# One fused attention and MLP kernel, five engines in a written-out order: the order of all operations and the identity products replaced

## The chip, the cores and the metric

The kernel runs on one core of a Trainium2 chip. The metric is the device time of one execution in microseconds (us); the kernel before was run three times and its median is 237.82 us. Engines are named as in the profile: PE (TensorE, matrix products), DVE (VectorE), ACT (ScalarE), POOL (GpSimd) and SP (SyncE, which only issues DMAs here).

## The reference, cut to what matters

Each of 4 x 8 heads has a sequence of 768 positions of 64 numbers, cut into 8 blocks of 96. An 8 x 8 matrix P per head is normalised five times by rows and columns. Blocks of k and v are mixed with P, and each block of q attends to the mixed block of its own index alone. The result, 3072 tokens of 512 numbers, goes through an MLP with a leaky slope per hidden unit.

```python
for _ in range(5):
    P = np.exp(P - np.max(P, axis=-1, keepdims=True))
    P = P / (np.sum(P, axis=-1, keepdims=True) + 1e-09)
    P = P / (np.sum(P, axis=-2, keepdims=True) + 1e-09)
k_sorted = np.einsum('bhij,bhjcd->bhicd', P, k_b)
v_sorted = np.einsum('bhij,bhjcd->bhicd', P, v_b)
attn = softmax(scale * q_b @ k_sorted_b.T)          # inside one block of 96
x = (attn @ v_sorted_b) -> [3072, 512]
h = x @ w_in                                        # [3072, 2048]
g = np.maximum(h, 0.0) + alpha * np.minimum(h, 0.0)
out = g @ w_out                                     # [3072, 512]
```

## The kernel before

The kernel has two layers. The function `bass_sinkhorn_attn__then__act_prelu_kernel` adds some 1230 operations to a graph (`G.add`), each with the buffers that it reads and writes; an operation is one instruction, or a few that belong together. The table `SEQ` then gives the order: it lists the number of every operation once, and `arrange` puts each at the end of its engine's list as it comes. A letter behind a number (p, a, d) chooses POOL, ACT or DVE for an operation that may run on several. `emit` writes each engine's list with the semaphore waits that the buffers ask for. Every engine works its list strictly in order. The durations and priorities that `G.add` also takes are read by neither `arrange`, `warm` nor `emit`: with the table given, no instruction depends on them.

The table `WARM` puts identity products into PE's list: `89:14:y` means 14 products of the identity with itself, 512 columns each, ahead of operation 89, into the PSUM bank `psY`. Their results are never read (line 808 is their product; four more of them are an operation of the graph).

The work, by the lines that the profile shows:

- q, k and v of batch 0 and both weight matrices are loaded by DMAs that POOL issues (L397, L419, L908 for w_in in four pieces, L913 for w_out in two). They follow each other in one queue.
- P is normalised on DVE and ACT in a chain of small operations (L518 to L532). The product L539 spreads the result over partitions, and DVE makes from it the block matrix BDK (L543).
- For batch 0, the products L600 transpose q and mix k, in six groups of 16 each; L653 copies v into an order that the products L674 can read, in eight copies that POOL or DVE may do; ACT and DVE bring results out of PSUM into QTz, KT and VS (L372).
- Attention of block g: scores (L715 in the first eight blocks, L712 later), the row maximum on DVE (L721), in the first eight blocks a second round of products with the maximum subtracted (L736, L727) and the exponential ET (L759); later the exponential per head (L748) and a DMA transpose of its result, issued by SP. Then the output product (L768), its division by the sum (L776, L779) and a transpose to xT, by PE (L794) or by a DMA from SP.
- The later batches' k and v are mixed through KSz and VDz (copies L616 and L658, products L629 and L669), their q comes through QN (L401) and DMA transposes.
- MLP: L823 computes a group of 128 hidden units for 192 tokens (the first two chunks, two blocks each) or 384 tokens (later), four products to a group, into one of three PSUM banks at first and one of two later. ACT takes the negative part (L833), DVE puts both parts together into hT (L836), which frees the bank. L863 computes 128 tokens of the output in four groups of four products; the first two of these need the first half of w_out. ACT or DVE copies the result out (L372), and SP stores it.

Of the kernel before, what the change touches and what calls it, by code (L numbers as in the profile page):

```python
# [7 lines left out]
AP = bass.AP  # L8
# [17 lines left out]
VSL = 4  # L26
# [6 lines left out]
89:14:y 79:8:y 93:2:y 104:2:y 158:6:y 118:1:y 128:4:y 162:1:y 153:3:h 205:1:y 207:1:y  # L33
# [3 lines left out]
0 7 11 2 3 1 4 8 9 22 42 28 14 43 44 45 46 19 47 18 5 48 49 50 15 51 39 52 53 6 54 55 25 56 138 57 58 23 29 59 12p  # L37
60 61 130 62 63 64 31 65 32 66 37 13 67 68 89 69 83 81 70 84 71 87 131 10 91 88 85 132 72 40 73 90 74 133 75 86 76
41 77 82 134 78 79 92 26 80 147 93 148 102 94d 103a 104 95 105a 100 98 96a 99a 97d 109d 106p 35 111d 112d 108p 34
16 101a 36 38 33 107p 158 149 114 115d 146 110p 118 250p 159 116 248p 119a 120 113p 121d 124 30 117d 160 135 125a  # L40
249p 254p 24 136 161 122 137 144 150 126 127a 143 123d 145 128 151 129d 253p 247d 20 17 152 162 21 163 164 141 153
177 154 140 155 165 156 142 166d 184 157a 167 185 196 193 168 186 169 194 197 195 199 198 187 202 170 27 203 205
200 204 188 201 214 206 220 215 217 189 218 207 221 219 222 226 216 229 190 227 223 230 273 228 224 171 208 231 225
235 191 236 238 192a 237 232 239 261 251 262 209 313p 233 252a 240 210 263 347p 211 139 255 241 270 234 212 403 264
256a 213d 291 404 301d 271 242 175 259 292 258p 274 260a 257p 272 265 352p 267 243 266 279 244 311p 293 280 268
300p 281 282 269 312p 294 245 174 304d 285 310p 246d 275 286 351p 283 287 284 338 348p 302 339 295 305p 303a 314
288 296 315 306 289 316 340 307a 290 176 297 320 341 317 276 318 178 321 319 298 322 379 299a 308 380 323 179 309a
342 326 324 343 349 344 327 381 350a 325 328 345 353 382 346d 329 354d 332 330 383 333 331 357 277a 334 180 335
572p 384 361 385 336 402 373 362 337 360p 358a 183 363 419 359d 574p 386 364 420 391p 367 365 374 355p 368 366 421
356d 573p 182 388 387d 370 389d 395p 375 577p 369 371 392 390p 435 372 393a 429 394p 436 396 430 376 397d 437 422  # L50
445p 431 432 578p 377d 398 446p 181 453 399d 447p 405 454 449p 433 438 455 465 448p 400 434 459 401a 466 456 460
451 461 457 406 467 452d 483 458 415 423 450d 477 462 475p 478a 172 468 424 413 495 476d 463 407 425 484 418 378
496 408 411 464 481 409d 412 482a 486 485 426 479p 549 487 427d 497 480p 488 439 506p 507 440 492 508d 509p 489 414
441 493 498 511 494 505p 490 442 525 443a 491 516 510p 512a 417 526 513 517 278 535p 537 518 514 469 550 571p 527
515 416 470 519 471 536p 522 538d 520 528 472 561 523 521 539 473a 562 543 540a 499 524 428 544 541 551 563 500 501
546 534 542d 502 545 575 503a 597 576d 474 547 555 548 529 556 606 530 558 564 607a 612p 557 552 609p 531 559 608p
560 610 553a 579 444 638p 613d 611a 582 598 580 532 635 583 591 637d 599 581 570 636d 585 584 592 586 600 533a 639
587 588 640a 626 589 614 646 627 644 641 615 565 590 593 643 628 566 645 616 617 642d 620 567 618 629 594 621 619
622 677 595a 504 568 623 678 569a 659 624 601 410 660 662 602 679 554 603 663 625 661 604 668 605a 680 718p 704 669
671 713p 705 714p 664 672 706 673 665 670 630 719 631 674 666a 632 752p 707 648 686 675 649 633 676 692 687 667  # L60
748p 634a 716d 596 720a 739 688 681 650 689 749d 715p 717d 698 690 647 750 691 658 699 693 751a 700 652 701 173 740
721 778p 702 682 753p 694 703 722 741 723 695 754 724 755d 696a 742 727 683 725 779 726 728 733 729 768 848d 730
854p 769 777p 756 731 812p 780a 708 732 654 734 757 709 782d 770 655 783 758 735 784d 657 762 710 813p 771 759 763
651 743 764 760 814 736 849p 711 815a 761 656 781d 803 744 847p 785 737d 684 850p 804 765 786 853p 653 788 766 805
767 789 787 794 745 797 806 838 798 816 839 772 697 817a 790 795 738 799 818 840 746 791 773 796 774 820 819d 775
800 792a 807 801 851 793 826 821 802 852a 841 822 873 823 874 832 824 747 881 833 827 888p 882a 834 846 875 828 825
808 855 884d 685 809 885 835 856 883d 911p 886a 857 842 887p 836 829 912p 837 712 909 843 830a 861 858 831 862 910a
901 863 876 867 859 860 889 811 902 913 890 864 891 868 865 844 903 869 914d 866 895 915 904 896 892 897 870 893
810 916a 894 877 871a 917 935 776 918 898 936 920 899 919 937 921 900 878 879 929 926 880 961 927 905 962 930 922
938 928 981 963 931 923 906 907 845 932 943 933 964 987 934 944 982 924d 908 988 939 946 945 983 989 940 941 949  # L70
# [960 lines left out]
```

## Time and profile before

| what | value |
|---|---|
| three runs | 237.7, 237.82, 238.86 us |
| span of the profiled execution (first to last instruction) | 236.6 us |
| PE busy, granted clock | 229.2 us, 1.000 |
| DVE busy | 169.8 us |
| ACT busy | 151.6 us |
| POOL busy | 73.0 us |
| moved by DMA | 31.36 MB in 71453 packets |

The profiled execution gives its span; what lies around the span is not in it, and the median of the runs is 1.2 us above it. In the profile a matrix product's time includes its latency, so neighbours overlap: the distance of two starts is what a product costs PE. A row of the timeline gives the start, the time, engine, line, what is written and read, and in brackets the idle time before it with what ended it.

### The profile page before, as it was taken

What the parts mean: (1) busy time and instruction counts of PE and PEld (TensorE: products, weight loads), DVE (VectorE), ACT (ScalarE), POOL (GpSimd) and SP (SyncE); (2) the same over time, 40 slices, a digit from 0 to 9 for tenths busy, and PEclk for the clock granted to TensorE, in tenths of its full rate; (3) what the DMA queues carried; (4) which work ended last, traced back from release to release, by engine and by line L of the source; (5) the groups of instructions that cost most, each with busy time, mean ns of one, the idle gap of its engine ahead of it and who ended that gap; (6) DMA issues with size and microseconds to landing.
All of it is one profiled execution on the core that took longest, in us unless ns stands there. A gap on an engine that the chain in (4) does not pass through costs nothing.

```text
span 236.6 us, 6266 instructions
## 1 busy us (share of the span) xinstructions
PE 229.2 (97%) x2532; PEld 142.2 (60%) x2532; DVE 169.8 (72%) x354; ACT 151.6 (64%) x423; POOL 73.0 (31%) x139
## 2 busy tenths in 40 slices
PE   7998998999999999999999999999999999999995
PEld 3446676687666666556566665655555555555543
DVE  4748796989899997868887667676766587744350
ACT  4475265587887988886678786756864646453332
POOL 7958812915659620338590020000000000000000
PEclk9999999999999999999999999999999999999999
DMA  5999999999989999899998796542642323400033
GB/s 96 212 213 168 211 217 202 179 209 158 191 88 167 152 120 173 119 210 166 165 111 114 188 164 135 98 90 52 125 92 82 97 50 79 140 0 1 0 133 135
DMA packets 71453, 31.36 MB, mean 133 GB/s; under 512 B 64504, under 2 KB 65280, under 8 KB 71424
## 3 DMA queue, kind: packets, MB, share of 16 engines
q0 software_dynamic: 22896, 13.63, 42.0%
q1 hardware_dynamic: 48528, 17.33, 37.8%
q8 instruction: 20, 0.33, 0.5%
q14 instruction: 9, 0.07, 0.1%
HBM read 27.28 MB, written 6.29 MB: 142 GB/s over the span
## 4 chain that ended last, share of the span: by engine, by line
PE 76%; DMA 17%; POOL 6%; issue 1%; ACT 0%; POOLq 0%
PE psH L823 31%; PE psYP L863 28%; DMA w_out_bf<-in_moe_w_out_dram 10%; PE psS L863 3%; PE psS L712 3%; DMA VST<-in_v_dram 3%; PE psO L768 3%; PE psYP L669 2%; DMA ET<-Esb 2%; PE psYP L629 1%; DMA QTz<-QN 1%; POOL w_in_bf L908 1%; PE psO L863 1%; PE psS L727 1%; POOL VDz L456 1%; PE psO L794 1%
## 5 line engine op out<-in xcount | busy, mean ns | idle before, releaser
L836 DVE SCALAR_TENSOR_TENSOR hT<-t,omaT,psH 128x384 bf16<-128x384 f32 (+1 forms) x139 | 77.4, 571 | 36.6 <-ACT t L833 35.1
L823 PE MATMUL psH<-xT,w_in_bf 128*128 128x384 bf16 (+1 forms) x556 | 96.9, 311 | 0.0
L833 ACT ACTIVATE t<-psH 128x384 f32<-128x384 f32 (+1 forms) x139 | 63.1, 461 | 50.3 <-PE psH L823 49.2
L863 PE MATMUL psYP<-w_out_bf,hT 128*128 128x512 bf16 x336 | 83.2, 379 | 1.3 <-DMA w_out_bf<-in_moe_w_out_dram 1.3
L823 PEld LDWEIGHTS psH<-xT,w_in_bf 128*128 128x128 bf16 x556 | 49.5, 98 | 28.9 <-DVE hT L836 1.6
L863 PEld LDWEIGHTS psYP<-w_out_bf,hT 128*128 128x128 bf16 x336 | 30.8, 98 | 30.1 <-DMA w_out_bf<-in_moe_w_out_dram 1.8
L748 ACT ACTIVATE Esb<-psS,nf 96x96 bf16<-96x96 f32 x192 | 46.1, 345 | 2.0 <-DVE nf L721 2.0
L721 DVE TENSOR_REDUCE nf<-psS 96x8 f32<-96x768 f32 x24 | 22.8, 951 | 6.4 <-PE psS L712 6.0
L658 POOL COPY VDz<-VST 64x192 f32<-64x192 f32 x39 | 20.4, 524 | 20.3 <-DMA VST<-in_v_dram 16.6
L779 DVE TENSOR_TENSOR xq<-psO,rec 96x512 bf16<-96x512 f32 x31 | 21.2, 683 | 0.5
L401 POOL DMA_DIRECT2D QN<-in_q_dram x24 | 19.8, 833 | 3.3 <-DMA QTz<-QN 2.7
L616 POOL COPY KSz<-KS 64x256 f32<-64x256 f32 x28 | 11.1, 397 | 31.6 <-PE psYP L629 19.8
L712 PEld LDWEIGHTS psS<-KT,QTz 128*96 128x96 bf16 x192 | 12.1, 124 | 3.3 <-DMA QTz<-QN 0.2
L768 PEld LDWEIGHTS psO<-VS,ET 112*128 112x128 bf16 x248 | 11.1, 98 | 3.6 <-ACT ET L759 0.2
L808 PE MATMUL psYP<-identb 128*128 128x512 bf16 x40 | 12.8, 453 | 0.4 <-ACT identb L372 0.4
L372 ACT ACTIVATE VS<-psYP 112x512 bf16<-112x512 f32 x15 | 10.3, 687 | 4.2 <-PE psYP L669 2.2
L768 PE MATMUL psO<-VS,ET 112*128 112x65 bf16 x248 | 12.7, 194 | 0.0
L712 PE MATMUL psS<-KT,QTz 128*96 128x96 bf16 x192 | 12.6, 208 | 0.0
L372 ACT ACTIVATE KT<-psYP 128x512 bf16<-128x512 f32 x15 | 9.0, 599 | 2.8 <-PE psYP L629 1.8
L669 PEld LDWEIGHTS psYP<-BDV,VDz 128*128 128x128 bf16 x192 | 8.2, 98 | 2.7 <-POOL VDz L658 0.4
L372 ACT ACTIVATE outstg<-psYP 128x512 f32<-128x512 f32 x13 | 7.7, 604 | 3.2 <-PE psYP L863 3.2
L669 PE MATMUL psYP<-BDV,VDz 128*128 128x64 bf16 x192 | 9.5, 193 | 0.2 <-POOL VDz L658 0.2
(137 smaller groups left out, 198.8 us busy)
## 6 DMA issues: line engine op xcount, KB each, us to landing
out_dram<-outstg SPq DMA_DIRECT2D x23, 256.0 KB, 2.5
KS<-in_k_dram POOLq DMA_DIRECT2D x3, 768.0 KB, 13.3
QN<-in_q_dram POOLq DMA_DIRECT2D x24, 96.0 KB, 4.4
w_in_bf<-in_moe_w_in_dram POOLq DMA_DIRECT2D x4, 512.0 KB, 17.3
w_out_bf<-in_moe_w_out_dram POOLq DMA_DIRECT2D x2, 1024.0 KB, 23.9
VST<-in_v_dram POOLq DMA_DIRECT2D x4, 384.0 KB, 17.6
hT<-in_q_dram POOLq DMA_DIRECT2D x1, 768.0 KB, 7.6
VST<-in_v_dram POOLq DMA_DIRECT2D x1, 768.0 KB, 11.1
```

Source lines behind the costliest of these rows:

```text
L372: return e.activation(o, i, ACTF.Copy) if e is nc.scalar else e.tensor_copy(o, i)
L658: G.add(SHIFT, lambda e, o2=o2, i2=i2: e.tensor_copy(o2, i2), {"dve": 424, "pool": 525}, r=vst, w=[("VDz", u % VSL, th)], prio=prio)
L669: inst = e.matmul(AP(t, off + dd * 64, [[row, 128], [1, 64]]), AP(VDz, (u % VSL * 4 + dd // 2) * 256 + dd % 2, [[VSL * 1024, 128], [2, 128]]),
L712: inst = e.matmul(o, AP(QTz[n], hp * 3072 + h4 * 768 + i * 96, [[6144, 128], [1, 96]]), AP(KT[n], (h4 * 8 + i) * bk, [[ld, 128], [64, 2], ...
L721: G.add(DVE, lambda e: e.tensor_reduce(AP(nx, 0, [[8, 96], [4, 2], [1, 4]]), AP(psX, 0, [[1024, 96], [512, 2], [96, 4], [1, 96]]), AxisLis ...
L748: inst = e.activation(AP(Esb[me], p * 128, [[1024, 96], [64, 2], [1, 48]]), AP(psX, (p // 4) * 512 + (p % 4) * 96, [[1024, 96], [48, 2], [ ...
L768: inst = e.matmul(AP(psZ, hp * 512 + h4 * 68, [[1024, 128], [1, 65]]), AP(ET[me] if far else ET[m], pos(h4, hp) * 96, [[800, nk], [1, 128] ...
L779: G.add(DVE, lambda e: e.tensor_tensor(out=AP(xq[me], 0, [[512, 96], [256, 2], [64, 4], [1, 64]]), in0=AP(psZ, 0, [[1024, 96], [512, 2], [ ...
L823: inst = e.matmul(AP(pt, poff, [[1024, 128], [1, n]]), AP(w_in_bf, kt * DFF + ft // 2 * 256 + ft % 2, [[KT_TILES * DFF, 128], [2, 128]]), ...
L833: G.add(ACT, lambda e: e.activation(AP(t1[tb], 0, [[384, 128], [1, n]]), AP(pt, poff, [[1024, 128], [1, n]]), ACTF.Relu, scale=-1.0), t_ac ...
L836: G.add(DVE, lambda e: e.scalar_tensor_tensor(out=AP(hT, ft * RING + tok % RING, [[FT_TILES * RING, 128], [1, n]]), in0=AP(t1[tb], 0, [[38 ...
L863: inst = e.matmul(AP(bank[0], bank[1], [[1024, 128], [1, n]]), AP(hT, ft * RING + tok % RING, [[FT_TILES * RING, 128], [1, 128]]), AP(w_ou ...
```

## The change

The two tables SEQ and WARM are replaced by new ones, and many durations in `G.add` by others. All operations, loads and buffers stay. In the diff below, SEQ is cut to the first line of each; of the durations two are shown.

```diff
 WARM = """
-89:14:y 79:8:y 93:2:y 104:2:y 158:6:y 118:1:y 128:4:y 162:1:y 153:3:h 205:1:y 207:1:y
+79:7:y 118:8:y 156:1:i 202:1:q 291:1:y
 """

 SEQ = """
-0 7 11 2 3 1 4 8 9 22 42 28 14 43 44 45 46 19 47 18 5 48 49 50 15 51 39 52 53 6 54 55 25 56 138 57 58 23 29 59 12p
...
+0 7 2 10 3 1 4 11 12d 5 8 42 43 9 6 44 45 138 46 47 26 48 25 49 50 131 35 51 40 52 53 54 55 56 57 58 59 60 61 62
...
-        G.add(PE, s1, 395, r=kt_keys + qt_keys + [("xq", 1)] * (g == 2),
+        G.add(PE, s1, 357 if far else 215, r=kt_keys + qt_keys + [("xq", 1)] * (g == 2),
...
-                5000 if g < 18 else 3100, r=[("Esb", me)], w=[("ET", me), ("turned", g)], prio=prio, dma=(d_e[me], 0))
+                950, r=[("Esb", me)], w=[("ET", me), ("turned", g)], prio=prio, dma=(d_e[me], 0))
```

WARM holds 43 identity products before and 18 now (with the four of the graph, 47 and 22). The new file is one line longer ahead of all its functions, so that a line of it is one higher than the same line before: L824 now is L823 before.

At PE's start, before, the row of psS products that multiply bz is a burst of small products, and psS, psH and psO<-identb,hT transpose q:

```order
L889 MATMUL psS<-bz 32x32 x130
L808 MATMUL psYP<-identb 128x512 x14
L600 MATMUL psS<-identb,hT 64x64 x16
L600 MATMUL psH<-identb,hT 64x64 x32
L600 MATMUL psO<-identb,hT 64x64 x16
L600 MATMUL psS<-identb,hT 64x64 x16
L600 MATMUL psO<-identb,hT 64x64 x16
L808 MATMUL psYP<-identb 128x512 x8
L539 MATMUL psYP<-Pb,sel 128x8 x8
```

The same place of PE's list now:

```order
L890 MATMUL psS<-bz 32x32 x130
L601 MATMUL psH<-identb,hT 64x64 x16
L601 MATMUL psS<-identb,hT 64x64 x32
L601 MATMUL psO<-identb,hT 64x64 x32
L809 MATMUL psYP<-identb 128x512 x7
L540 MATMUL psYP<-Pb,sel 128x8 x8
```

The 14 identity products ahead of the q products are gone; between these and the spreading of P stand seven instead of eight, and one of the six q groups has gone behind the spreading.

On DVE, behind the making of BDK, before (KT is mixed k, VST holds v as loaded, VS is mixed v, nm the row maximum):

```order
L543 TENSOR_TENSOR BDK<-mkh,psYP 128x128
L372 CAST KT<-psH 128x32x2x8
L642 COPY KT<-KT 128x32x8
L653 COPY hT<-VST 128x48x4
L482 TENSOR_REDUCE mkhV<-identf 128x8
L653 COPY hT<-VST 128x48x4 x2
L479 TENSOR_REDUCE mkjV<-identf 128x8
L459 MEMSET ET 128x16
L476 TENSOR_REDUCE mkj<-identf 128x8
L372 CAST VS<-psO 112x64x8
L721 TENSOR_REDUCE nm<-psH 96x8
```

And now:

```order
L544 TENSOR_TENSOR BDK<-mkh,psYP 128x128
L373 CAST KT<-psO 128x32x2x8
L460 MEMSET ET 128x16
L373 CAST KT<-psO 128x32x2x8
L373 CAST KT<-psH 128x32x2x8
L654 COPY hT<-VST 128x48x4 x4
L643 COPY KT<-KT 128x32x8
L373 CAST VS<-psO 112x64x8
L654 COPY hT<-VST 128x48x4 x2
L722 TENSOR_REDUCE nm<-psH 96x8
```

DVE takes three casts of KT instead of one and six copies of v instead of three; POOL's copies of v fall from five to two, and three of its four loads of w_in and the first of w_out now stand behind these two. Masks that DVE made here before are made earlier or later.

On PE, ahead of the first product with w_out, before:

```order
L715 MATMUL psS<-KT,QTz 96x96 x8
L768 MATMUL psO<-VS,ET 128x65 x8
L823 MATMUL psH<-xT,w_in_bf 128x192 x8
L823 MATMUL psYP<-xT,w_in_bf 128x192 x4
L808 MATMUL psYP<-identb 128x512
L736 MATMUL psS<-QTz,KT 112x96 x8
L727 MATMUL psS<-identb,nm 112x96 x8
L823 MATMUL psYP<-xT,w_in_bf 128x192 x4
L823 MATMUL psH<-xT,w_in_bf 128x192 x8
L863 MATMUL psYP<-w_out_bf,hT 128x512 x4
```

And now:

```order
L716 MATMUL psS<-KT,QTz 96x96 x8
L630 MATMUL psYP<-BDM,KSz 128x64 x8
L769 MATMUL psO<-VS,ET 128x65 x8
L824 MATMUL psH<-xT,w_in_bf 128x192 x8
L630 MATMUL psYP<-BDM,KSz 128x64 x8
L737 MATMUL psS<-QTz,KT 112x96 x8
L728 MATMUL psS<-identb,nm 112x96 x8
L824 MATMUL psYP<-xT,w_in_bf 128x192 x4
L824 MATMUL psH<-xT,w_in_bf 128x192 x4
L864 MATMUL psYP<-w_out_bf,hT 128x512 x4
```

From the start to this product PE's list holds, before, 40 products of L823, 32 each of L715, L736 and L727, 24 of L768, 8 of L794 and none of L629. Now it holds 64, 48 each, 40, 16 and 24: six more groups of the MLP, two more blocks of attention and three groups of the next batch's k.

The two lists of SP hold the same DMAs in another order of transposes and stores; those of POOL the same loads, with the later batches' loads among other copies than before.

More of the change, by code (lines that the diff above doesn't have):

```diff
@@ L40 @@
[L40 to L49, printed above, removed]
@@ L633, in prep_k @@
         if b:
-            G.add(PE, f, 250, r=[("KSz", u % 3, hp) for hp in range(2)] + [("BDM", b)], w=keys, prio=prio)
+            G.add(PE, f, 232, r=[("KSz", u % 3, hp) for hp in range(2)] + [("BDM", b)], w=keys, prio=prio)
         else:
-            G.add(PE, pairs(KS[n], 0, u, BDK, 0, 512, bank), 372, r=ks + [("BDK", 0)], w=keys, prio=prio)
+            G.add(PE, pairs(KS[n], 0, u, BDK, 0, 512, bank), 254, r=ks + [("BDK", 0)], w=keys, prio=prio)
         ld, bk = 4 * NB * BK0, BK0
```

209 lines of the change are left out of this document (110 added, 99 removed).

## The prediction

> **What bounds the kernel now.** I read the page first: its span, the busy times, and the busy share of PE slice by slice.
>
> ```profile
> span 236.6 us, 6266 instructions
> PE 229.2 (97%) x2532; PEld 142.2 (60%) x2532; DVE 169.8 (72%) x354; ACT 151.6 (64%) x423; POOL 73.0 (31%) x139
> PE   7998998999999999999999999999999999999995
> ```
>
> PE is full from about the seventh slice (36 us) to the last one. The share of busy time alone says little, so I read next the windows of 5 us (columns: the stretch, its length, then busy time and instructions of PE, PEld, DVE, ACT and POOL, the granted clock, the DMA share, GB/s).
>
> ```profile
> 25.00:30.00 5.00, 5.00 (x74) 3.36 (x72) 3.98 (x12) 1.72 (x4) 4.54 (x9) 1.00 1.13 212
> 30.00:35.00 5.00, 4.98 (x74) 4.12 (x72) 4.54 (x12) 2.76 (x9) 0.52 (x1) 1.00 1.14 217
> 35.00:40.00 5.00, 3.72 (x57) 2.82 (x56) 2.96 (x10) 2.85 (x8) 0.00 (x0) 1.00 1.20 200
> 40.00:45.00 5.00, 5.00 (x85) 3.98 (x85) 4.67 (x14) 3.14 (x9) 4.65 (x9) 1.00 1.36 200
> 75.00:80.00 5.00, 5.00 (x60) 3.18 (x58) 4.92 (x10) 4.70 (x16) 4.77 (x9) 1.00 1.37 149
> ```
>
> From 40 us on PE has no gap; the last hole is the 1.28 us in 35 to 40. DVE is nearly as full between 40 and 90 us (4.67, 4.92 of 5), and in 35 to 40 it is the emptiest (2.96). The timeline names the places.
>
> ```profile
> 2.80 5.62 PE L808 MATMUL psYP<-identb 128*128 128x512 bf16 x14 [0.37 <-ACT identb L372]
> 8.93 0.44 PE L600 MATMUL psS<-identb,hT 64*64 64x64 bf16 x16 [0.52 <-DMA hT<-in_q_dram]
> 9.20 0.67 PE L600 MATMUL psH<-identb,hT 64*64 64x64 bf16 x32
> 9.71 0.42 PE L600 MATMUL psO<-identb,hT 64*64 64x64 bf16 x16
> 10.57 1.90 PE L808 MATMUL psYP<-identb 128*128 128x512 bf16 x8
> 12.43 0.37 PE L539 MATMUL psYP<-Pb,sel 32*128 32x8 bf16 x8
> ...
> 28.71 0.83 PE L823 MATMUL psH<-xT,w_in_bf 128*128 128x192 bf16 x8
> ...
> 36.40 1.04 PE L863 MATMUL psYP<-w_out_bf,hT 128*128 128x512 bf16 x4 [1.27 <-DMA w_out_bf<-in_moe_w_out_dram]
> ```
>
> So the run has two parts. Up to 36.40 us PE waits for loads and for the chain of the first blocks and fills up with identity products. From the first output product of the MLP (L863) on it works without a gap to the end. The operations are the same in both kernels, so behind that product PE has a fixed amount of work less what was done ahead of it. The end is then the time of the first L863 plus the work that is left behind it, plus new gaps.
>
> **Term 1: work that moves ahead of the first L863.** In the order of before, 40 products of L823 stand ahead of it, with 32 each of L715, L736 and L727, 24 of L768 and 8 of L794. Now it is 64, 48 each, 40 and 16, and 24 of L629 that were all behind it. Groups run back to back here, so each step is the distance of two starts:
>
> ```profile
> 46.64 0.38 PE L715 MATMUL psS<-KT,QTz 64*96 64x96 bf16 x8
> 46.95 0.41 PE L629 MATMUL psYP<-BDM,KSz 128*128 128x64 bf16 x8
> 47.19 0.41 PE L768 MATMUL psO<-VS,ET 112*128 112x65 bf16 x8
> 47.44 0.83 PE L823 MATMUL psH<-xT,w_in_bf 128*128 128x192 bf16 x8
> 48.10 0.40 PE L629 MATMUL psYP<-BDM,KSz 128*128 128x64 bf16 x8
> 48.43 0.41 PE L736 MATMUL psS<-QTz,KT 64*112 64x96 bf16 x8
> 48.77 0.61 PE L727 MATMUL psS<-identb,nm 96*112 96x96 bf16 x8
> 49.21 0.83 PE L823 MATMUL psH<-xT,w_in_bf 128*128 128x192 bf16 x8
> 49.88 1.03 PE L863 MATMUL psYP<-w_out_bf,hT 128*128 128x512 bf16 x4
> 50.74 0.34 PE L794 MATMUL psO<-identb,xq 96*128 96x96 bf16 x4
> 51.00 0.38 PE L715 MATMUL psS<-KT,QTz 64*96 64x96 bf16 x8
> ```
>
> Six more groups of L823 at 0.33 (two in 47.44 to 48.10) are 1.98 us; two of L715 at 0.31, 0.62; two of L736 and L727 at 0.34 + 0.44, 1.56; two of L768 at 0.25, 0.50; two of L794 at 0.26, 0.52; three of L629 at 0.24, 0.72. The sum is **5.9 us**. The identity products need no term of their own: all 47 of before and all 22 of now stand ahead of the first L863, and what they cost there is in the next term.
>
> **Term 2: when the first L863 comes.** First the start. The run of 14 products is gone, so PE stands idle from the end of the burst (about 2.4 us) until q lands, and the transposing products of q at 8.93 are its first real work. The 14 products show what an unwarmed PE costs: 5.62 / 14 = 0.40 us each, against 0.22 later (1.90 for eight, the last one's tail of 0.38 in it). Five groups of q products now stand ahead of seven identity products, and those ahead of the product of L539 that spreads the mixing matrix. A q group takes 0.26 us warm (two in 9.20 to 9.71); unwarmed I bound it by that and twice that, and take 0.42, nearer the upper end since the large products nearly double: 2.1 us for five (1.3 to 2.6). Seven identity products at 0.40 are 2.8. L539 starts at 8.93 + 2.1 + 2.8 = 13.8, say 14.0 with the switch, and not at 12.43.
>
> The Trainium skill ("TensorE: Matmul & The Clock Gate", sections on the clock gate and on why it matters) speaks against this edit: keep TensorE busy for 4 us without a gap, and leave no idle gap over some 3 us. By it the array would still be at half rate when q lands and turn full one to two windows of about 3.4 us later, by estimate 12.3 to 15.7. The trace's step from 0.40 to 0.22 us agrees with it.
>
> What the late L539 costs depends on v, which lands at 16.6, and on the copies that follow it:
>
> ```profile
> 16.71 1.97 POOL L653 COPY hT<-VST 128x192 f32<-128x192 f32 x3 [2.49 <-DMA VST<-in_v_dram]
> 18.54 0.88 POOL L401 DMA_DIRECT2D QN<-in_q_dram x1
> 21.28 0.51 POOL L653 COPY hT<-VST 128x192 f32<-128x192 f32 x1
> 24.43 0.69 DVE L372 CAST VS<-psO 112x512 bf16<-112x512 f32 x1 [0.92 <-PE psO L674]
> 25.39 0.42 PE L768 MATMUL psYP<-VS,ET 112*128 112x65 bf16 x8
> L653 DVE COPY hT<-VST 128x192 f32<-128x192 f32 x3 | 1.0, 398 | 0.2 <-DMA VST<-in_v_dram 0.2
> ```
>
> In before the last copy of v ends on POOL at 21.8, behind a DMA issue and two other copies. Now POOL does two and DVE six. On DVE: BDK ends at 14.0 + 0.4 + 0.3 = 14.7; the first K group is in PSUM at 15.55; three casts at about 0.66 take it to 17.5; four copies at about 0.3 (0.398 alone, less overlap) to 18.7; the pad of KT, one cast and two more copies to 20.4. That is 1.4 earlier than 21.8, late L539 included. Two row maxima and two casts behind it (0.9 and 0.65 each) bring the last cast of VS to 23.5, against 24.43 + 0.69 = 25.1. From L768 at 25.39 to the first L823 at 28.71 before needs 3.3 us; now a mixing block of 0.78 (L736, L727) stands in between as well. So the first L823 is at 23.8 + 3.3 + 0.8 = **27.9**.
>
> Between that and the first L863, DVE decides. The first L863 now stands behind the sixteenth group of L823; groups share three banks, so this one waits for the thirteenth result of L836 on DVE. The order shows on DVE from the first L823 to there: 13 of L836, 3 of L721, 3 of L776, 3 of L779, one cast of KT, and 8 small ones.
>
> ```profile
> L836 DVE SCALAR_TENSOR_TENSOR hT<-t,omaT,psH 128x192 bf16<-128x192 f32 x27 | 10.2, 405 | 1.3 <-ACT t L833 0.9
> L721 DVE TENSOR_REDUCE nm<-psS 96x8 bf16<-96x768 f32 x7 | 6.6, 950 | 0.8 <-PE psS L715 0.8
> L779 DVE TENSOR_TENSOR xq<-psO,rec 96x512 bf16<-96x512 f32 x31 | 21.2, 683 | 0.5
> L776 DVE RECIPROCAL rec<-psO 96x8 f32<-96x8 f32 x31 | 6.2, 198 | 1.5 <-PE psO L768 1.1
> L372 DVE CAST KT<-psYP 128x512 bf16<-128x512 f32 x4 | 2.7, 682 | 0.0
> ```
>
> 13 x 0.405 + 3 x 0.95 + 3 x 0.198 + 3 x 0.683 + 0.68 = 11.4, and the small ones about 1.9: 13.3 us, some 0.5 less for overlap of neighbours. From 27.7 DVE is through at 40.5, and with one L823 behind it the first L863 is at **40.9**, 4.5 later than 36.40. PE alone would be there after 16 x 0.33 + 3 x 0.31 + 3 x 0.78 + 3 x 0.25 + 2 x 0.26 + 3 x 0.24 + 2 x 0.22 = 11.0 us, at 38.9; the other 2.0 are its waits for DVE. w_out does not decide any more: it lands at 36.4, unless its issue moves. It does, behind two copies of v, to about 20 us, but the queue then still holds the loads ahead of it (DMA share 1.13 and 1.14 in 25 to 35). I cost that at nothing; a hole in the queue would cost its own length, up to 40.9 hidden.
>
> **Sum.** 4.5 - 5.9 = -1.4. Behind it, DVE in before sat idle for 2.0 in 35 to 40 and 0.3 in 40 to 45; a row that keeps DVE at work from 27.7 on brings it ahead there, and PE's short waits of 40 to 55 shrink. I add -0.4 (0 to -1.5). Bounds of the start: q groups and an earlier clock give -0.8, a later clock +0.5. **-1.8 us** (-3.6 to -1.2 within this case): a span of 234.8. The median of the runs, 237.82, is 1.2 above the span, so the forecast is **236.0 us**.
>
> The orders on SP (transposes) and the later loads change too. I cost them at nothing: counted in steps of this kind, 8.4 us of PE work or more stand between the scores of a block behind the first eight and its output product in both orders, against 0.95 (L721) + 8 x 0.345 at most (L748) + 3.3 for the transpose, 7.0. Without that cover each late block would cost the difference.
>
> ```profile
> L748 ACT ACTIVATE Esb<-psS,nf 96x96 bf16<-96x96 f32 x192 | 46.1, 345 | 2.0 <-DVE nf L721 2.0
> ET<-Esb SPq DMA_TRANSPOSE x24, 3.3
> ```
>
> **Rivals.** (a) DVE eats the gain: if it waits for PE and ACT for 1 us or so in its stretch from 27.7, or runs on at the limit behind 40.9, the first L863 slips toward 42 and the time stays within 0.5% (1.2 us, about what a measurement can tell here): 237.5. For it speaks DVE's 4.92 of 5 at 75 to 80. Chance 0.28. (b) Slower, by the clock: if PE is not at full rate when the eight identity products ahead of the v products begin (about 16.7), these take 3.2 instead of 1.7 and the blocks behind them run at up to twice their steps. L823 then starts at about 30.5 to 33, and its first groups still run slow: +2.6 to +6 on the forecast, 239.5 or so in the milder half, up to 242. Against it: PE is at work from 8.93 to 14.0 almost without a gap, and in before the products turned fast about 4.9 us after the first large one at 2.80. It decides at about 16 us. Chance 0.12. (c) PE is fed: DVE overlaps better than I sum, the first L863 comes at 38.9, and 2.5 - 5.9 = -3.4 or more follows: 234.4 at once, 232.9 with the later gaps gone too. Chance 0.10. (d) A transpose or load of a later block comes late in the new order, +1.5 to +3 on the forecast and more: 239.2. Chance 0.05.
>
> **Numbers.** Forecast 0.45; (c) 0.10; (a) 0.28; (b) and (d) 0.17. Faster by over 0.5%, below 236.6: 0.55. Within: 0.28. Slower: 0.17. The range leaves out the upper part of (b) and the end of (c): 233.0 to 239.2.
>
> **What would show it.** The first L863 near 41 us with 64 L823 ahead of it (sooner: (c)); L539 near 14 and 0.4 us identity products ahead of it; DVE over 4.6 of 5 in every window from 28 to 40; PE without gaps from about 55 on. I am wrong if L823 starts after 30 or if gaps of PE stand behind 60 us.

## The result and the profile after

The changed kernel takes 251.15 us (median of four runs, 250.34 to 252.13); the kernel before, run beside it on the same chip, 238.34 us. The ratio is 1.0548, with a 95% interval of 1.0507 to 1.0589: slower by 12.8 us, where 1.8 us faster was forecast. The ratios below leave disturbed executions out, so a time that is named with a ratio is the ratio times the median of the kernel before beside it (238.0 to 238.3 us); of fix_88 only one undisturbed run is left, and the profile of rest_88 was of a disturbed one and isn't used.

The page of the changed kernel (PE's busy tenths and its granted clock in 40 slices of 6.3 us):

```profile
span 250.3 us, 6163 instructions
PE 226.1 (90%) x2478; PEld 140.9 (56%) x2507; DVE 174.4 (70%) x371; ACT 147.0 (59%) x418; POOL 67.4 (27%) x127
PE   1699999999399999989785999999999999999995
PEclk9999999999859999999999999999999999999999
```

PE is busy for 226.1 us of 250.3, before for 229.2 of 236.6 (54 products fewer are recorded: the 25 identity products that were left out, and 29 of L864 whose records are missing from this trace). Holes stand in the slices at 63 to 69 us and from 106 to 137 us, and the clock falls behind the first of them. The windows show the same (busy times of PE, PEld, DVE, ACT, POOL; granted clock; DMA share; GB/s):

```profile
30.00:35.00 5.00, 4.75 (x74) 3.84 (x73) 5.00 (x13) 2.86 (x10) 3.38 (x7) 1.00 1.12 214
35.00:40.00 5.00, 5.00 (x101) 4.39 (x99) 4.93 (x14) 3.68 (x10) 2.37 (x5) 1.00 1.20 200
60.00:65.00 5.00, 4.12 (x34) 2.23 (x32) 4.95 (x9) 3.09 (x12) 1.97 (x4) 1.00 1.33 174
65.00:70.00 5.00, 1.55 (x12) 1.01 (x13) 0.57 (x2) 0.00 (x0) 0.00 (x0) 0.74 0.96 157
70.00:75.00 5.00, 4.78 (x31) 2.46 (x30) 2.04 (x5) 3.06 (x11) 1.96 (x4) 0.58 0.99 157
105.00:110.00 5.00, 4.34 (x31) 2.07 (x30) 4.12 (x9) 3.14 (x11) 2.77 (x6) 1.00 1.23 170
120.00:125.00 5.00, 3.40 (x38) 1.89 (x37) 3.87 (x8) 3.94 (x12) 1.42 (x3) 1.00 1.09 140
130.00:135.00 5.00, 1.78 (x18) 1.04 (x16) 2.92 (x6) 1.74 (x8) 2.66 (x6) 1.00 1.12 132
```

The 35 to 40 window, where PE had a hole of 1.28 us before, is full: the start went as forecast. PE's timeline, first the start, then the first hole:

```profile
8.49 0.63 PE L601 MATMUL psH<-identb,hT 64*64 64x64 bf16 x16 [6.10 <-DMA hT<-in_q_dram]
10.77 2.67 PE L809 MATMUL psYP<-identb 128*128 128x512 bf16 x7
13.37 0.36 PE L540 MATMUL psYP<-Pb,sel 32*128 32x8 bf16 x8
28.17 0.83 PE L824 MATMUL psH<-xT,w_in_bf 128*128 128x192 bf16 x8
40.56 0.81 PE L864 MATMUL psYP<-w_out_bf,hT 128*128 128x512 bf16 x3
...
54.93 0.53 PE L713 MATMUL psS<-KT,QTz 128*96 128x96 bf16 x8 [0.35 <-ACT t L834]
63.72 0.53 PE L713 MATMUL psS<-KT,QTz 128*96 128x96 bf16 x8
68.45 0.60 PE L769 MATMUL psO<-VS,ET 112*128 112x65 bf16 x8 [4.21 <-DMA ET<-Esb]
```

The scores of block 8, the first of batch 1, come at 54.93. Its output product (L769) was to follow at 64.2 and waits 4.2 us for its transposed exponentials. SP, which issues the transposes in list order, shows why they are late; the kernel before first:

```profile
50.95 11.79 SPq L409 DMA_TRANSPOSE QTz<-QN  x5
62.79 1.29 SPq L753 DMA_TRANSPOSE ET<-Esb  x1
64.12 1.31 SPq L409 DMA_TRANSPOSE QTz<-QN  x1
```

And the changed kernel:

```profile
50.28 12.32 SPq L410 DMA_TRANSPOSE QTz<-QN  x5
62.64 1.31 SPq L754 DMA_TRANSPOSE ET<-Esb  x1
63.99 1.76 SPq L410 DMA_TRANSPOSE QTz<-QN  x1
66.48 4.90 SPq L754 DMA_TRANSPOSE ET<-Esb  x1
```

SP does the same at nearly the same times in both: five Q tiles until 62.6 or 62.8, then the exponentials of block 8. What moved is PE, which reaches this block's scores 2 us earlier than before (54.93 against 56.88), and POOL's loads of batch 2. POOL before:

```profile
41.84 0.56 POOL L435 DMA_DIRECT2D VST<-in_v_dram  x1
42.36 0.61 POOL L419 DMA_DIRECT2D KS<-in_k_dram  x1
56.28 0.53 POOL L435 DMA_DIRECT2D VST<-in_v_dram  x1
```

And now:

```profile
48.66 0.54 POOL L436 DMA_DIRECT2D VST<-in_v_dram  x1
53.32 0.53 POOL L436 DMA_DIRECT2D VST<-in_v_dram  x1
63.08 0.57 POOL L420 DMA_DIRECT2D KS<-in_k_dram  x1
72.88 0.83 POOL L402 DMA_DIRECT2D QN<-in_q_dram  x1 [8.65 <-DMA QTz<-QN]
73.76 1.67 POOL L659 COPY VDz<-VST 64x192 f32<-64x192 f32 x3
```

The 768 KB of batch 2's keys go out at 63.08 in place of 42.36, beside the transposes of 62.64 to 66.48. POOL then stands for 8.65 us at a QN load that may not overwrite its tile before the last Q tile is turned, and copies to VDz that PE needs (L670) stand behind it. In the chain of waits of the second stretch a Q-tile transpose, a QN load on POOL, the keys of batch 3 and a row maximum follow on each other:

```profile
104.09 6.35 DMA QTz<-QN
...
116.56 7.51 DMA QTz<-QN
...
124.61 0.82 POOL QN L402
125.43 6.63 DMA KS<-in_k_dram
132.08 0.28 DVE KSz L617
132.37 0.87 DVE nf L722
```

### The profile page after: what moved, and what is told of

Read it like the earlier page. It is cut to its first block, busy times and chain, and to the rows that moved or that the text cites. A ratio compares the mean times of both kernels' runs of the same rounds, so it can differ in the third digit from the quotient of the medians.

```text
span 250.3 us, 6163 instructions
## 1 busy us (share of the span) xinstructions
PE 226.1 (90%) x2478; PEld 140.9 (56%) x2507; DVE 174.4 (70%) x371; ACT 147.0 (59%) x418; POOL 67.4 (27%) x127
## 4 chain that ended last, share of the span: by engine, by line
PE 69%; DMA 15%; DVE 7%; ACT 4%; issue 2%; SPq 2%; POOL 0%; DVEq 0%; ACTq 0%; POOLq 0%
PE psH L824 26%; PE psYP L864 21%; DMA QTz<-QN 6%; PE psS L864 3%; DMA hT<-in_q_dram 3%; PE psO L769 3%; DMA KS<-in_k_dram 3%; PE psS L713 3%; DVE hT L837 2%; DMA ET<-Esb 2%; PE psYP L809 2%; ACT t L834 2%; PE psYP L670 1%; ACT Esb L749 1%; PE psYP L630 1%
## 5 line engine op out<-in xcount | busy, mean ns | idle before, releaser
L824 PE MATMUL psH<-xT,w_in_bf 128*128 128x384 bf16 (+1 forms) x556 | 100.3, 315 | 4.2 <-DVE hT L837 3.9
L834 ACT ACTIVATE t<-psH 128x384 f32<-128x384 f32 (+1 forms) x139 | 62.6, 464 | 64.0 <-PE psH L824 62.8
L864 PE MATMUL psYP<-w_out_bf,hT 128*128 128x512 bf16 x309 | 79.8, 382 | 1.9 <-ACT outstg L373 0.3
L824 PEld LDWEIGHTS psH<-xT,w_in_bf 128*128 128x128 bf16 x556 | 49.3, 99 | 36.2 <-DVE hT L837 9.5
L864 PEld LDWEIGHTS psYP<-w_out_bf,hT 128*128 128x128 bf16 x336 | 31.4, 98 | 30.4 <-issue 0.9
L659 POOL COPY VDz<-VST 64x192 f32<-64x192 f32 x34 | 17.7, 522 | 23.6 <-PE psYP L670 15.1
L769 PE MATMUL psO<-VS,ET 112*128 112x65 bf16 x248 | 12.9, 196 | 5.8 <-DMA ET<-Esb 5.8
L769 PEld LDWEIGHTS psO<-VS,ET 112*128 112x128 bf16 x248 | 11.0, 99 | 9.4 <-issue 4.3
L617 POOL COPY KSz<-KS 64x256 f32<-64x256 f32 x25 | 10.1, 405 | 19.9 <-PE psYP L630 13.8
L713 PE MATMUL psS<-KT,QTz 128*96 128x96 bf16 x192 | 12.6, 209 | 1.2 <-DMA QTz<-QN 0.7
L713 PEld LDWEIGHTS psS<-KT,QTz 128*96 128x96 bf16 x192 | 11.3, 125 | 4.0 <-ACT t L834 1.8
L670 PEld LDWEIGHTS psYP<-BDV,VDz 128*128 128x128 bf16 x192 | 8.5, 99 | 3.4 <-issue 0.3
L373 ACT ACTIVATE outstg<-psYP 128x512 f32<-128x512 f32 x12 | 7.0, 596 | 5.6 <-PE psYP L864 4.3
L373 ACT ACTIVATE VS<-psYP 112x512 bf16<-112x512 f32 x14 | 9.6, 686 | 1.1 <-PE psYP L675 0.8
L670 PE MATMUL psYP<-BDV,VDz 128*128 128x64 bf16 x192 | 9.8, 196 | 0.0
L864 PE MATMUL psS<-w_out_bf,hT 128*128 128x512 bf16 (+1 forms) x46 | 8.8, 324 | 0.1
## 6 DMA issues: line engine op xcount, KB each, us to landing
out_dram<-outstg SPq DMA_DIRECT2D x23, 256.0 KB, 2.6
VST<-in_v_dram POOLq DMA_DIRECT2D x4, 384.0 KB, 11.9
```

The source lines that it names most:

```text
L373: return e.activation(o, i, ACTF.Copy) if e is nc.scalar else e.tensor_copy(o, i)
L670: inst = e.matmul(AP(t, off + dd * 64, [[row, 128], [1, 64]]), AP(VDz, (u % VSL * 4 + dd // 2) * 256 + dd % 2, [[VSL * 1024, 128], [2, 128]]),
L713: inst = e.matmul(o, AP(QTz[n], hp * 3072 + h4 * 768 + i * 96, [[6144, 128], [1, 96]]), AP(KT[n], (h4 * 8 + i) * bk, [[ld, 128], [64, 2], ...
L769: inst = e.matmul(AP(psZ, hp * 512 + h4 * 68, [[1024, 128], [1, 65]]), AP(ET[me] if far else ET[m], pos(h4, hp) * 96, [[800, nk], [1, 128] ...
L824: inst = e.matmul(AP(pt, poff, [[1024, 128], [1, n]]), AP(w_in_bf, kt * DFF + ft // 2 * 256 + ft % 2, [[KT_TILES * DFF, 128], [2, 128]]), ...
L834: G.add(ACT, lambda e: e.activation(AP(t1[tb], 0, [[384, 128], [1, n]]), AP(pt, poff, [[1024, 128], [1, n]]), ACTF.Relu, scale=-1.0), 170 ...
```

## The experiments

The numbers are operations as SEQ lists them; each diff shows one engine's list. Theory 1 looked for PE's single waits, theories 3 and 5 for the loads behind them; theory 2 and 4 were the rivals of the moment.

**One wait at a time.** ks_earlier, on POOL:

```diff
-650 649 782 778 813 752 657 648 654
+650 649 648 782 778 813 752 657 654
```

> Edit: in the changed kernel, one entry of SEQ is moved: the last of the four loads of batch 3's keys (operation 648) goes from behind the load of QN head 6 (657), which waits for the last transpose of batch 2, to directly behind the third of these loads (649). Theory 1 (the loss is made of PE's waits for transposes and loads that stand in the in-order lists of SP and POOL at about 64, 123 and 131 us): the hole of 3.4 us at about 131 us goes, the other two stay, so 251.15 - 3.4 = 247.8 us, between 247.0 and 249. Theory 2 (the loss is in the start or in the identity products that are missing): nothing changes, 251 us.

Measured 1.0604 (1.0529 to 1.0679), 252.4 us: no gain. The hole at 131 went, the one ahead of it grew:

```profile
66.89 0.40 PE L769 MATMUL psO<-VS,ET 112*128 112x65 bf16 x8 [0.42 <-DMA ET<-Esb]
72.29 0.39 PE L670 MATMUL psYP<-BDV,VDz 128*128 128x64 bf16 x8 [1.95 <-POOL VDz L659]
...
124.73 0.40 PE L769 MATMUL psO<-VS,ET 112*128 112x65 bf16 x8 [3.40 <-DMA ET<-Esb]
```

The moved load went out at 114.60. A Q tile issued just ahead of it took 9.3 us to land in place of 7.5, and the exponentials behind that 7.6 in place of 5.8; PE's 3.40 us are the wait for the latter. The first two rows are of the stretch that this edit left as it was: here PE came to block 8 2.5 us later, after a start at half clock, waited 0.42 us for it and 1.95 us for VDz, and the execution took 250.1 us all the same.

et8_ahead, on SP:

```diff
-178 179 181 180 182 422 183
+178 179 180 422 181 182 183
```

> Edit: in the changed kernel, three entries of SEQ are moved, all of SP's list: the transpose of E of group 8 (422) directly behind its exponentials, and the transposes of Q tiles 3 and 4 (181, 182), which no group before 12 reads, behind it. SP then issues Q tiles 0, 1, 2, then E of group 8, then Q tiles 3, 4. Theory 1: the transpose is issued at about 58.5 in place of 62.6 us, PE's wait of 4.4 us at 64.0 shrinks below 1 us, the clock stays full, and so the 2.9 us that PE lost at half rate from 68.45 to 74.23 go too: 251.15 - 6.3 to 7.3, 243.9 to 244.9 us. Theory 2 (the hole is only a symptom: what comes behind it would wait anyway for the Q tiles or for DVE, as the rest of the plan is 4 us ahead of its loads): less than half comes back, 248 to 250 us.

Measured 1.0528 (1.0465 to 1.0591), 250.6 us. Block 8's wait was gone, and PE stood a little later:

```profile
64.36 0.41 PE L769 MATMUL psO<-VS,ET 112*128 112x65 bf16 x8
74.85 0.59 PE L670 MATMUL psYP<-BDV,VDz 128*128 128x64 bf16 x8 [7.04 <-POOL VDz L659]
```

hole_warm, in WARM:

```diff
+423:20:h
```

> Edit: in the changed kernel, 20 identity products are added to WARM ahead of the first matmul that waits for E of group 8 (operation 423); nothing else. They fill PE's wait from 64.0 to 68.4 us with 20 x 0.215 = 4.3 us. If the half clock from 67.4 to 74.2 us is caused by the idle stretch: clock full throughout, and the 5.8 us of work that ran at half rate take 2.9 us less: 251.15 - 2.9 = 248.2 us. If the clock drop has another cause (it came 3 us into the hole by chance, or it costs nothing because PE waits anyway): 251 us or above.

Measured 1.0618 (1.0541 to 1.0695), 252.7 us, with the clock at 1.00 throughout its profile:

```profile
64.89 4.49 PE L809 MATMUL psH<-identb 128*128 128x512 bf16 x20 [0.49 <-DVE hT L837]
75.84 0.39 PE L670 MATMUL psYP<-BDV,VDz 128*128 128x64 bf16 x8 [3.17 <-POOL VDz L659]
```

So the idle stretch did cause the half clock, and holding the clock is worth nothing here. In et8_ahead and hole_warm the second product L670 of batch 2 comes at 74.85 and 75.84 us (74.54 in the changed kernel). Block 8's wait and the half clock lie beside another chain that ends later: keys of batch 2, last Q tile, QN load, copy to VDz, L670. Theory 1's way of adding waits up had failed.

**Which load.** pool2, on POOL (its copies in between stand as they were):

```diff
-402 ... 475 450 404 447 416 448 449 480 573 479 571 577 418
+402 404 ... 475 450 447 448 449 480 573 479 571 577 416 418
```

> Edit: in the changed kernel, two entries of POOL's list are moved: the load of batch 2's keys (404) from behind three copies to VDz that wait for PE to directly behind the first half of batch 2's values (402); and the first load of batch 2's QN (416), which waits for the last transpose of batch 1, from between the copies to VDz of batch 2 to directly ahead of the next such load (418), behind these copies. Theory 3 (PE's order is fine; what fails is that these two entries make the transposes share the DMA engines with 768 KB of keys from 63 to 71 us and shut the copies to VDz in behind a load that waits until 73 us): the transpose of E of group 8 takes about 3.9 us in place of 5.7 and lands at 66.5, PE waits 2.4 us in place of 4.2, too short for the clock to drop, 251.15 - 1.8 - 2.9 = 246.5 us, and no new wait at 72. Theory 4 (PE's own order reaches group 8 and batch 2 some 5 us before any order of the loads can serve it): PE waits as long as before, 250 to 252 us.

Measured 1.0611 (1.052 to 1.0702), 252.6 us. The copies to VDz were free now, but the keys went out at 49.2, just ahead of the first Q tile, and that took 12.6 us to land, at 62.4: not with the keys (57.6), but with the second half of the values, in flight from 53.3 to 62.3:

```profile
62.51 0.84 PE L713 MATMUL psS<-KT,QTz 128*96 128x96 bf16 x8 [7.96 <-DMA QTz<-QN]
```

pool2_et8 is that with et8_ahead:

> Edit: that of pool2 (keys of batch 2 and its first QN load on POOL) and that of et8_ahead (on SP the transpose of E of group 8 ahead of Q tiles 3 and 4) together. In et8_ahead PE's wait went from 64 to 67.5 us and grew to 7.2 us, behind a copy to VDz that stood on POOL behind the QN load. Theory 3: with both taken away no wait over 1 us is left from 60 to 80 us and the clock stays full: 251.15 - 4.4 - 2.9 = 243.9 us, between 243 and 245. Theory 4: a wait of 3 us or more stays somewhere between 60 and 80 us, on the values or keys of batch 2 themselves: 248 to 252 us.

Measured 1.0662 (1.0616 to 1.0707), 253.8 us. all5 adds ks_earlier and, on SP:

```diff
-534 570 428 600 629 474 444 554 680 707 667 504 742
+534 570 428 444 474 600 629 554 504 680 707 667 742
```

> Edit: that of pool2_et8, and for the second stretch: on POOL the last quarter of batch 3's keys (648) behind its third (649), ahead of a QN load; on SP the transposes of Q tiles 1 and 2 of batch 2 (444, 474) directly behind that of tile 0, and tile 3 (504) ahead of E of group 16. Theory 3: the holes at 107 to 111 (1.4 us), 123 (1.8) and 131 us (3.4) go as well: 243.9 - 6.6 = 237.3 us, the changed kernel then being 0.5 to 1 us ahead of the one before. If each hole only moves on to the next operand that lands: 241 to 246 us.

Measured 1.0885 (1.0827 to 1.0943), 259.1 us. Theory 3 was wrong as it stood: each place to which the keys or the transposes were moved made other transposes late. What the misses had in common became theory 5: a transpose beside a bulk load is the one that is late. ks2_late sends the keys only when the transposes of batch 1 are through, on POOL:

```diff
-475 450 404 447 416 448 449 480 573 479 571 577 418
+475 450 447 448 449 480 416 404 573 479 571 577 418
```

> Edit: in the changed kernel, on POOL the first QN load of batch 2 (416) and the load of batch 2's keys (404) are moved behind the copies to VDz of batch 2 (480), the keys last, so that they go out only when the last transpose of batch 1 has landed. Theory 5: with no keys in flight the transpose of E of group 8 (issued at 62.6) lands 3.1 us later, at 65.7 us in place of 68.3, and the last Q tile (issued at 64.0) at about 67.5 in place of 72.6; PE waits 1.7 us at 64 us in place of 4.2 and the clock stays full: 251.15 - 2.6 - 2.9 = 245.6 us. Theory 4: the wait stays, or its place is taken by one of the same size before 80 us: 249 us or more.

Measured 1.037 (1.0302 to 1.0438), 247.1 us. From issue to landing, the transposes of exponentials issued from 55 to 72 us, two in each kernel, took in the changed one:

```profile
DMA to landing us min/median/max: 5.7/7.3/9.0
```

And in ks2_late, where these two have no keys beside them:

```profile
DMA to landing us min/median/max: 2.9/3.0/3.1
...
77.94 0.40 POOL L617 COPY KSz<-KS 64x256 f32<-64x256 f32 x1 [6.34 <-DMA KS<-in_k_dram]
```

The next transpose there, issued at 72.53 with the keys in flight (71.04 to 77.88), took 6.2 us. The second row is the new wait: POOL stands at a copy of the late keys, with a copy to VDz behind it. ks2_late_ksz moves these copies, too:

```diff
-480 416 404 573 479 571 577 418 ... 412
+480 479 416 404 418 ... 412 573 571 577 574 572 578
```

> Edit: ks2_late, and the six copies to KSz of batch 2 (573, 571, 577, 574, 572, 578) moved on POOL behind the QN loads of batch 2, so that no copy to VDz stands behind a copy that waits for the late keys. In ks2_late PE's new wait of 2.0 us at 77 us was for such a copy to VDz (POOL stood from 71.6 to 77.9 us on the keys). If that is its only cause: 247.8 - 2.0 = 245.8 us. If PE only waits for the next operand: 247 us or more.

Measured 1.029 (1.0243 to 1.0337), 245.2 us, as expected: 5.9 us of the 12.8 are back, by entries of POOL alone. The keys and the QN load were moved together, so the share of each isn't known. ks2_late_et8:

> Edit: that of ks2_late and that of et8_ahead (on SP, E of group 8 ahead of Q tiles 3 and 4). Theory 5: E of group 8 lands at 62 to 63.7 us, no wait of PE over 1 us is left from 60 to 72 us, clock full: 251.15 - 4.4 - 2.9 = 243.9 us. Theory 4: 249 us or more.

Measured 1.0494 (1.0441 to 1.0546), 250.0 us: a miss. PE waited 5.4 us at 74 us for a copy to VDz, behind a POOL that stood 7.5 us at the late keys; ks2_late_ksz takes that away.

**The loads in the order of before.** before_ksz, meant as a control, and before_ks_late, on POOL:

```diff
-403 404 258 ... 305 572 402 360 ... 448
+403 404 258 ... 305 402 360 ... 448 572 574 573 577 578
```

```diff
-403 404 258 ... 305 402 360
+403 258 ... 305 404 402 360
```

> Control. Edit: the tables of the kernel before, in which the five copies to KSz of batch 2 on POOL (572, 574, 573, 577, 578) are moved behind the copies to VDz of batch 2 (448), at about 66 us; PE reads the first of them at about 86 us. No load moves. Every theory expects no change: 238.0 us within 0.5 us.

> Edit: before_ksz, and in it the load of batch 2's keys (404, 768 KB) moved on POOL from 42.4 to about 48.4 us, behind the last copy of batch 1 (305). The keys themselves are not needed before 66 us. Theory 5 (the transposes on SP and POOL's bulk loads share the DMA engines, and a transpose that is issued while a 768 KB load is in flight lands only about when that load has landed; the loss of the changed kernel comes from when this load stands against the transposes): the first Q tile, issued at 51, lands at about 62 us in place of 56.7, as in pool2 (62.4); PE waits 4.5 to 5.5 us at 57 us for it and loses another 1.5 to 3 us at half clock: 244 to 247 us. Theory 4 (PE's own order is what reaches its operands too early; the kernel before has the slack): 238 to 239 us.

Measured 1.0067 (1.0042 to 1.0092), 239.9 us, and 1.0128 (1.0066 to 1.019), 241.3 us. The control was none: with the copy 572 gone from its place, the second half of batch 2's values went out at 47.95 in place of 56.28, beside the Q tiles, and the first tile took 8.0 us in place of 5.8. That agrees with theory 5 on the order of before. The size for before_ks_late was wrong: the keys, issued 5 us later (47.22 against 42.12), landed at 55.4, as they had at 55.75. The QN loads ahead of them in POOL's queue landed until 50 us in both, so what was issued later did not get through later. That is argued from the landings; the 1.4 us between the two kernels, whose intervals overlap, are not explained by it. Nor is all of the control's loss the Q tile: PE's wait for it was 0.8 us, and its profiled execution also ran at 0.71 of the clock from 25 to 30 us.

**The start, and the second stretch.** Each of these takes the first entries of one SEQ and the rest in the order of the other:

```python
splice_start = after[:258] + rest of before      # first L864
splice_322   = after[:322] + rest of before      # 48 us
start_290    = after'[:290] + rest of before     # after' has 140 141 142 behind 20
rest_88      = before[:589] + rest of after      # up to operation 570, 88 us
after_to_88  = after[:573] + rest of before      # up to operation 570
fix_88       = ks2_late_ksz up to 570 + rest of before
```

> Edit: the first 258 entries of the changed SEQ, up to and with the first FFN2 group, and behind them all remaining operations in the order of the kernel before; the WARM of the change. If the start's forecast gain of 1.4 to 1.8 us is real and only the order behind it lost the time: 238.3 - 1.4 to 1.8 = 236.5 to 236.9 us. If the earlier start is given back at the next load that has to land (the four QN loads, landed at 50.9 us in both kernels): 238.3 us. If the start itself holds part of the loss: above 239 us.

> Edit: the first 322 entries of the changed SEQ (up to the loads of batch 2's values, at 48 us) and behind them all remaining operations in the order of the kernel before, so that the loads of batch 2 come first on POOL and its PE order follows; the WARM of the change. In splice_start PE waited 2.1 us at 45 us for the second half of w_out, which the changed POOL list issues 6 us later than before. Here the changed order covers that place. If the start's gain of 1.4 to 1.8 us holds through 48 us: 236.5 to 236.9 us. If it is given back at what the older order wants next from the loads: 238.3 to 241 us.

> Edit: the first 290 entries of the changed SEQ (46 us), with the three last QN loads of batch 1 (140, 141, 142) moved on POOL directly behind the clearing of their tiles, at about 33 us, and behind these entries the order of the kernel before, which issues the loads of batch 2 first; the WARM of the change. In splice_start (258 entries) PE waited 2.1 us for w_out at 45 us, and in splice_322 the keys of batch 2 went out at 50.8 us, beside the Q tiles. Neither stands here. If the start's gain holds once the loads stand as before: 236.5 to 236.9 us. If the loads' landing, not PE's order, sets when batch 1 can start: 238 to 240 us.

splice_start: 1.0136 (1.0099 to 1.0172), 241.3 us, with the wait for w_out at 47.42. splice_322: 1.0303 (1.0261 to 1.0344), 245.2 us; the keys went out at 50.8 and PE waited 5.2 us for the first Q tile. start_290: 1.0055 (1.0011 to 1.0099), 239.6 us, the best of the kernels with the changed start and still not ahead of before. Its PE:

```profile
46.03 1.04 PE L864 MATMUL psYP<-w_out_bf,hT 128*128 128x512 bf16 x4 [1.04 <-DMA w_out_bf<-in_moe_w_out_dram]
57.12 0.56 PE L713 MATMUL psS<-KT,QTz 128*96 128x96 bf16 x8 [0.85 <-DMA QTz<-QN]
```

With the loads as before, the earlier PE waits 1.9 us for w_out and the first Q tile, and starts block 8 at 57.12, before at 56.88. The gain of the start is given back there.

> Edit: the order of the kernel before up to and with the last Q-tile transpose of batch 2 (operation 570, entry 572, at about 88 us), and behind it all remaining operations in the changed order; at this place the two orders have done nearly the same operations. The WARM of before. If the changed order behind 88 us makes its own holes (in the changed kernel 0.5 + 0.9 us from 105 to 111, 1.8 at 123, 3.4 at 131): 238.3 + 6.6 = 244.9 us, between 243.5 and 246. If these holes are only what is left of the disorder at 64 us: 238 to 239.5 us.

Measured 1.0272 (1.0237 to 1.0307), 244.8 us against an expected 244.9: the order behind 88 us loses 6.5 us by itself.

> Edit: the order of ks2_late_ksz up to and with the last Q-tile transpose of batch 2 (570), and behind it all remaining operations in the order of the kernel before; the WARM of the change. This takes away both places of loss at once and keeps the changed start. If the two places are all of the loss: 245.8 - 4.2 (what ks2_late still waited from 105 to 130 us) - 1.8 to 3 (its profiled execution had its start at half clock from 25 to 28 us) = 238.6 to 239.8 us, and 236.9 us if the start's gain of 1.4 us is kept as well. If something else holds loss: above 241 us.

> Edit: the changed order up to and with the last Q-tile transpose of batch 2 (570), and behind it all remaining operations in the order of the kernel before; the WARM of the change. The counterpart of rest_88, which measured the changed order behind this place at 244.9 - 238.3 = 6.6 us. If the two stretches lose independently of each other: 251.15 - 6.6 = 244.5 us, between 243.5 and 246. If the order of the kernel before cannot be joined here without waits of its own, as fix_88 (245.5 to 250 us) suggests: 246 to 251 us.

fix_88 took 245.48 us in one run and 250.3 to 256.0 in the other three, after_to_88 1.0447 (1.0409 to 1.0485), 248.6 us: both missed what the sum of the parts asked for. In after_to_88 PE waited 2.6 us at 107 us, where neither parent waits over 1: the order of before can't be joined to the changed one at 88 us without a wait of its own. Its first stretch has the entries of the changed kernel, and in this execution PE waited 0.8 us for block 8 and 6.1 us for VDz:

```profile
65.51 0.40 PE L769 MATMUL psO<-VS,ET 112*128 112x65 bf16 x8 [0.82 <-DMA ET<-Esb]
75.05 0.59 PE L670 MATMUL psYP<-BDV,VDz 128*128 128x64 bf16 x8 [6.09 <-POOL VDz L659]
```

One order, two pictures, and ks_earlier gave a third. What differs is how long ahead of the keys SP issued the exponentials of block 8: 0.4 us ahead they took 5.7 us to land (changed kernel), 1.6 us ahead 3.1 (after_to_88), 2.1 us ahead 3.2 (ks_earlier). The last Q tile, issued next and awaited by POOL's QN load, took 8.6, 9.6 and 5.6 us, and L670 came at 74.54, 75.05 and 72.29: its time goes with the Q tile, not with block 8.

**The identity products.** b_few, in the WARM of before:

```diff
-89:14:y 79:8:y 93:2:y 104:2:y 158:6:y 118:1:y 128:4:y 162:1:y 153:3:h 205:1:y 207:1:y
+89:6:y 79:3:y 158:2:y 118:1:y 128:1:y 162:1:y 153:1:h 205:1:y 207:1:y
```

> Edit: SEQ of the kernel before, and in its WARM 17 identity products in place of 43 (89:6, 79:3, 158:2 and one each at 118, 128, 162, 153, 205, 207), about the number that the change leaves. If the products that the change takes out fill only idle time and the clock holds without them: 238.3 us within 0.5 us. If their number is what holds the clock in the first 30 us: 1 to 3 us slower, 239.3 to 241.3 us.

Measured 1.0101 (1.0061 to 1.0141), 240.4 us:

```profile
20.00:25.00 5.00, 2.50 (x77) 2.11 (x73) 3.51 (x6) 2.02 (x3) 4.34 (x11) 0.91 1.08 179
25.00:30.00 5.00, 5.00 (x64) 3.57 (x65) 1.94 (x6) 1.50 (x2) 4.54 (x8) 0.50 1.12 210
```

In the order of before the identity products help to hold the clock: without 26 of them PE stood idle for 2.25 us until 24.95, the clock was at half from 25 to 30 us, and the first L824 came at 32.28 in place of 28.71. All five of its runs have a mean clock of 0.964 to 0.986, those of the kernel before beside it 0.993 to 1.000. Their number alone doesn't decide it: before_ksz, with all 43, had a hole of 1.75 us and a dip there too.

## Why the prediction was wrong, point by point

**The start held.** L540 came at 13.37 (14.0 forecast) behind seven identity products at 0.38; the first L824 at 28.17 (27.9), the first L864 at 40.56 (40.9), DVE full from 30 to 40 us (5.00, 4.93). Neither (a) nor (c) came about. PE was 2 us ahead at 55 us, as the sum of -1.4 and -0.4 had it, with as much real work done (one block of L769 less, one group of L670 more). The sum's own bounds, -0.8 and -1.5 or +0.5 and 0, give -3.7 to -0.9 us and not the -3.6 to -1.2 that stands there; that decides nothing here.

**The step that failed** is the last of the sum: "The orders on SP (transposes) and the later loads change too. I cost them at nothing". The PE work between the scores of block 8 and its output product was 9.3 us (54.93 to 64.24), the 8.4 or more that I had counted. Against it stood not 7.0 but 13.4 us: the exponentials were ready after 3.6 (58.5 us, as in the estimate); they then waited 4.1 us in SP's list behind five Q tiles; and the transpose took 5.7, not 3.3. Before, the need was 11.0 us (scores at 56.88, landed at 67.88) against 11.9 of PE work: 0.9 us left.

```profile
56.88 0.52 PE L712 MATMUL psS<-KT,QTz 128*96 128x96 bf16 x8
...
68.75 0.41 PE L768 MATMUL psO<-VS,ET 112*128 112x65 bf16 x8
```

From 0.9 us to spare to 4.1 too few are 5 us: 2.6 are PE work that the new order took out from between, 1.7 are a longer wait in SP's list, since PE came 2 us earlier and SP didn't, and 0.6 are the transpose. The median of 24 transposes stood for the one that mattered, the wait in SP's list was left out, and the cover of before was not measured where it was thinnest. This wait alone did not make the loss: et8_ahead took it away and gained nothing. The loads, the other half of the term, did more: moving POOL's entries gave 5.9 us back (ks2_late_ksz).

**Where the 12.8 us are.** 5.9 us come back when POOL's loads and copies of batch 2 are reordered (ks2_late_ksz, 245.2), and 6.5 us are lost by the order behind 88 us alone (rest_88). That leaves 0.4 us, but the two can't simply be added: fix_88 and after_to_88 asked for the sum and missed it, and the profile of ks2_late_ksz, which changes nothing behind 88 us, is 5.6 us ahead of the changed kernel's at the second L670, 4.4 at 104 us and 6.8 at the end. The first is shown down to its cause: the keys of batch 2 in flight beside the transposes, and the copies shut in behind a QN load. Of the second only the place is shown. The chain from 104 to 132 us above reads the same way (transposes of 6.4 and 7.5 us beside the loads of batch 3, and POOL's last load of keys behind a QN load), and in ks_earlier a load of keys moved beside two transposes made each 1.8 us longer. But the two edits tried there (ks_earlier, all5) brought nothing, and none took the loads away from the transposes. So the cause there stays argued.

**Where the forecast gain went.** PE could run ahead to 55 us because the keys of batch 2 were out of the way until 63 us. With these loads as before (start_290) the same start waits for w_out and the Q tile; with them late, the transposes behind pay. This is read from the runs and not tested by itself. I had read PE's gapless stretch from 40 us as PE work alone, while the loads landed just in time for it.

**The rivals.** (d), a late transpose or load, was the right mechanism at a chance of 0.05 and a price of 1.5 to 3 us. It was 15 us on the forecast, as I priced one block and not a list that keeps all behind it waiting. (b), the clock in the start, didn't decide the result: the granted clock was 1.00 from 15 to 65 us in the changed kernel's profile, and the eight identity products ahead of v ran at full rate. But it was near. Of the 15 kernels profiled here that have the changed start, two (ks_earlier, ks2_late) ran at 0.79 and 0.50 from 25 to 30 us, with the first L824 at 30.65 and 32.25 in place of 28.1 to 29.8. The half clock at 67 us costs nothing of its own (hole_warm).

## What to carry to other kernels

Where an order is changed, follow each in-order list that issues DMAs, entry by entry, and compare the work that covers each transfer with its own issue-to-landing time there, ahead of its queue: a median over all of them hides the thin places. A gap-free engine may be fed just in time, and then work done earlier is given back at the next load. Waits that stand one after the other on one engine don't add up until it is known which chain ends last; an edit that removes one of them and changes nothing is the sign.

## What the runs showed of the hardware

Transposes lose against bulk loads. A transpose of E took 2.9 to 3.1 us with no bulk load beside it (ks2_late) and 5.7 to 9.0 with 768 KB of keys in flight (the changed kernel); the first Q tile took 12.6 us behind the same load and half of the values (pool2), and 4.5 and 5.8 us in the changed kernel and in the one before. It isn't the keys alone: two Q tiles of the changed kernel, issued at 53.48 and 55.08 with half of the values (53.32 to 60.20) and other Q tiles in flight, took 9.3 and 8.5 us.

The length of one wait doesn't tell whether the clock falls. Every wait of PE of 3.40 us or more behind 40 us ended at half clock: 3.40 us in ks_earlier, 4.21 us in the changed kernel, there for 6.8 us (0.74 and 0.58 in its windows from 65 to 75 us: 2 x 5 x (0.26 + 0.42)). Of the shorter ones some kept it at 1.00, as 3.17 us (hole_warm) and 3.21 us (the changed kernel at 131 us) did, and some didn't: 2.07 us in pool2 at 132 us (0.50 from 135 to 137 us), and 0.37 and 1.91 us with a few products between them in splice_start at 45 us. The Trainium skill ("TensorE: Matmul & The Clock Gate", "Why this matters for your kernels") asks for no idle gap over some 3 us. The longer waits here agree with it; the shorter ones show that to stay below 3 us wasn't enough.
